# Two layers of linear attention and two of dilated window attention: a new order, new engine choices and new buffer numbers

## The chip, the cores and the metric

The kernel runs on one core of a Trainium2 chip. The metric is the time of one launch in microseconds, as the device reports it; before the change the median of three runs is 329.12 us. One execution was also taken with the hardware profiler.

A core has engines that run side by side, each through its own list of instructions in order: PE multiplies matrices (PEld is its loading of weights), DVE works elementwise, ACT applies functions and scales, POOL does small clears and copies, and SP issues the DMA transfers. An instruction that must wait for another engine or for a transfer holds up everything behind it in its own list.

## What is computed

```python
x = A_x                                    # 1 x 2048 x 512, bf16; 32 heads of 16
x = x + A(layernorm(x)); x = x + B(layernorm(x))
x = x + A(layernorm(x)); x = x + B(layernorm(x))

def A(x):                                  # linear attention with learned features
    q, k, v = heads(x @ wqkv)
    phi = lambda u: concat(softmax(u @ w_phi), softmax(-(u @ w_phi)))
    kv, z = sum_s(phi(k) * v), sum_s(phi(k))
    return (phi(q) @ kv / (phi(q) @ z + 1e-6)) @ wo

def B(x):                                  # 8 keys per row, at distances 0, 2, .. 14
    q, k, v = heads(x @ wqkv)
    return (softmax(q . k[window] / 4) @ v[window]) @ wo
```

## The kernel before

The 2048 rows are cut into four blocks of 512 (`x[0]` to `x[3]`), each of four tiles of 128 rows. All of `x` and all the weights stay in the core's memory. A method of the class `_Fast` writes each stage down as a list of small steps, one list for each stage, block and engine. The stages are:

- `s_loads` and `s_load_B`: the input loads, all on SP. `x[0]` comes in four tiles (L337), the other blocks whole (L340); the K and Q parts of A's weights as raw halves (L349, the tile `wraw`), its V part straight into `WA` (L343); `WoA` in four pieces (L353); B's weights `WB` in three parts (L418) and `WoB` in four (L422). A DMA also waits until the eighth one ahead of it has landed.
- `s_fold`: the raw Q and K weights are transposed on PE (L386), copied (`wT`), multiplied with the block diagonal of `w_phi` (L396) and copied into `WA`.
- `s_ln_first` and `s_norm`: layer norm. Statistics of a tile on DVE (L515, L516), logarithm and exponential on ACT (L450, L453), the shift on DVE (L457), the scaling into `xn` on DVE (L466) or ACT (L468), then the transposition to `xnT` on PE (L482, and a copy) or by DMA (L473).
- `s_a1`: K features and V. Matmuls L616 and L628, two exponentials L622 for each tile, V's eviction into `vaug`, sums by halving (L649 to L662), reciprocal (L668, L669), multiplication L674, and the sum over the rows L691, for all blocks into one bank.
- `s_a2`, `s_akv`: Q features (L721, L729) and their sums (L737, L743, L744); the finished sum is copied to `kvT`, transposed (L767) and spread into `ZM` and `R` (L776, L780). This is the one place in a layer A where every block of K must be finished.
- `s_a3`, `s_a4`, `s_out`: denominators, the product with `R`, the output projection (L543), the residual sum, and the squares (L563) for the next layer norm.
- `s_b1`, `s_b2`, `s_b3`: layer B. Projections L951; V is laid out for its window by 16 DMAs a block (L1012, the tile `Vg`); products `prod` (L1043), the sum over a head on PE (L1050), exponentials L1057, sums L1066, weights `PT` (L1078), products `pav` (L1105), their sums on PE (L1114), projection and residual as above.
- `s_e1` to `s_e4`: the last block of the last layer B is computed in another way, with block diagonal Q (`Qbd`), small matmuls (L1278, 128 to 144 for a tile, and L1322, 128 for a tile), masks L1304, normalization L1349 and transposes L1366. Its V goes through DRAM (L1232 to L1243) into the memory of `WA`, and into `Vx`.
- `s_flag`: counts that decide whether a second, general path has to run. DVE computes the flag (L1388 to L1405), every engine reads it (L1412), and here it never asks for the path.

Three tables set how these lists are merged, and the diff touches only these.

`_ORDER` is a list of 1488 numbers in base 36. Each names one of the 682 lists, and `run` takes the next step of that list and writes its instructions down. The order of instructions on every engine and on SP's queue is the order in this table:

```python
for w in _ORDER.split():
    key = self.names[int(w, 36)]
    i = n.get(key, 0)
    n[key] = i + 1
    self.threads[key][i]()
```

`_CHOICE` holds a digit for each of 380 steps that two engines could do; 1 stands for DVE, 0 for ACT. Most are evictions of a PSUM bank (`copy`, L203 on DVE, L205 on ACT) and the scaling of the layer norm. In the residual sum (`res`) 0 is DVE (L556), and 1 is one more matmul on PE, with the identity (L546), and an eviction on ACT (L553). In `bev` 1 means no eviction at all: DVE reads the bank itself.

`_SLOTS` gives each temporary its buffer by number: `ps` for the eight PSUM banks, `big` for eight buffers of 4096 elements a row, `med` for sixteen of about 2048, `t2` for six small ones. A step that writes a buffer waits until the last reader of its former content is done.

Of the kernel before, what the change touches and what calls it, by code (L numbers as in the profile page):

```python
# [75 lines left out]
6j 6a 6e 9a 9b 9c 9b 6r 9b 9b 83 7y 7y 84 9f 9b 8d 7z 6s 6s 6s 9f 9h 6s 6t 6t 88 89 9i 7y 6s 6t 4w 4x 83 83 6q
6q 7y 6q 85 88 4y 88 8b 83 9g 87 86 81 b2 9j 9k 88 8c 9m 9n 8f 9w 9x 82 9w 9w a1 6r 9z 69 6u 9w 80 6u 6v 8a 6u
6v 6x 6v 4w 6w 6q 6u 6v 6y 9m 4v 4z 4z 6z 4v 70 71 4z 4z 70 70 9y 72 7x 73 72 74 70 75 72 72 76 9o 9r 9r 50 51
8f 50 50 72 52 76 78 8e 8e 50 53 77 54 9r 9u 79 7a 9m 9p 7b 8f 9s 9t 55 8e 56 57 8f 55 58 55 55 59 8g 8g 8g 8e
a0 8g 57 57 a3 9r 5a 57 9v 9m 9q 5b a3 57 5b 8h 8h 5c b3 5e 5d 5f 5g 7x 9l a2 b0 b0 a3 b1 b1 b1 8g 8h b1 b3 b3  # L80
b6 b3 b7 bz c0 c0 a4 a4 a4 a3 a4 a5 a5 bz c0 c0 bz d3 b4 bz c0 c0 c0 c0 8f 8i b0 b1 a4 8i 8i 8i a5 as at b0 b1
b1 bx ap a2 b5 b1 ap 8j 8k 8j 8j 8l 8m 8j bx 8n 8o a3 a6 a2 a6 8p 8o 8o 8o bx aq aq aq aq by by by 8q 8t 8r 8s
as 8q a2 as as bx a6 a7 8q 8q a7 by 8u bz 8q a6 8u 8w 8y by by aw av 8v a7 8x a8 a7 aa ap ap a9 ab ac b8 b8 au
ac i7 ac ac by by bx b8 b8 ad aq aq af aq aq ag b9 bo c0 8z ah b8 bb bb ae ae ae ae ai be ax ae ai aj an c1 be
bc bb bc bc ak ax bc bb bc bc bc bc ac ac am ax ac ax ay al ac bg be bm bm ao bm bm bj bn bn bn bn bn bn ar ax
az az az bu bu bu bu az bn bn c2 bv bj bj by bu bj bu ba ba ba ba bp bh bp bp c1 bq bk bs br be c1 c1 bu bu bu
bp bj bf bl bl bl c2 c2 bi bl bv bw c2 c2 c2 bu bw c2 bw c2 bt bw c1 c7 c2 c8 c9 c9 ca c9 cb fp c3 cc cb ca ce
# [12 lines left out]
il ik fn fo gr gr il gw gx iq io iq iq gv gw gv gw gv gv ip iq iv dx dx fk fm fm gy gz h2 is gw gw ir it h2 iw  # L100
# [12 lines left out]
_SLOTS = {  # L113
    "med": (
        "0123456789abcdef346aff72ffc3105f92b4de6a7fd92b317ef99962c0517dbf2e3abf6925cd13e273a31dad901d74235cdb"
        "f72a94d35c017b9264acf31d08"
    ),
    "ps": (
        "0123124350123021456715604156734153267234701623047237452365001230210345672135304675261473045672350146"
        "1401230453013042567103651251741023452036714302310345031240230435406703203501467012012457245201240310"  # L120
        "3245602750235102563740130473024567142362047540123640760437034563745101021345067241301456701236204531"
        "7024560124567326452016435735601247351204561203460750264012312301203405367136731421432102324567467556"
        "47554701213740542010"
    ),
    "big": (
        "012345670123456012345617234561720351724361720436170425361725362503421034210354276"
    ),
    "t2": (
        "0123455500111123334555555555555555000002123402222222221314504555545555444455223000000145523333333333"
        "333333301045234102"  # L130
    ),
    "pp": (
        "640620202020"
# [1967 lines left out]
```

## Time and profile before

| | us |
|---|---|
| median of three runs | 329.12 |
| lowest, highest of them | 328.67, 1771.92 |
| span of the profiled execution, first to last instruction | 327.7 |
| busy in it: PE, DVE, ACT, POOL | 308.8, 296.3, 278.1, 39.1 |

One of the three runs took 1771.92 us; the median isn't moved by it. The span leaves out what lies around the program, 1.0 us and more by the two other runs. In the profile a line such as L1043 is a line of the kernel, and `out<-in` are the tiles' names without their buffer numbers. Times in a timeline count from the start of the span. A busy PE is not always a PE at its peak, as matmuls overlap. "Issue" as a releaser stands for a wait that the profile can't put down to another instruction.

### The profile page before, as it was taken

How to read it: one execution, taken by the hardware profiler on the slowest of the kernel's cores; microseconds unless marked ns; L12 is line 12 of the kernel's file. 1: busy time of each engine (PE TensorE's matmuls, PEld its weight loads, DVE VectorE, ACT ScalarE, POOL GpSimd, SP SyncE). 2: the span in 40 equal slices, each digit the busy share in tenths (PEclk: the TensorE clock that was granted, in tenths of full speed). 3: DMA queues.
4: the chain of work that ended last, by engine and by line, in shares of the span. 5: the costliest groups of instructions: out<-in, count | busy, mean ns of one | idle time of the engine just before them, and what ended most of it. 6: DMA issues, size and time to landing. Idle time of an engine off the chain costs nothing.

```text
span 327.7 us, 8877 instructions
## 1 busy us (share of the span) xinstructions
PE 308.8 (94%) x3542; PEld 153.5 (47%) x3574; DVE 296.3 (90%) x456; ACT 278.1 (85%) x640; POOL 39.1 (12%) x64
## 2 busy tenths in 40 slices
PE   7999999899999999999999999789999999986993
PEld 3644456444444454444444455543545444443441
DVE  6899995989999999999999999599898999999493
ACT  4999989999789977999999999799898866987360
POOL 6000000000020006000000000000040395210000
PEclk9999999999999999999999999999999999999799
DMA  7964300023677979679991200050588997549814
GB/s 203 341 162 90 108 2 4 2 68 81 144 172 140 132 149 158 108 131 131 145 121 28 40 0 4 4 141 9 145 147 121 192 136 131 135 83 176 158 67 137
DMA packets 45793, 36.41 MB, mean 111 GB/s; under 512 B 30832, under 2 KB 41136, under 8 KB 45744
## 3 DMA queue, kind: packets, MB, share of 16 engines
q1 hardware_dynamic: 45216, 35.75, 56.2%
q8 instruction: 30, 0.49, 0.7%
q14 instruction: 19, 0.16, 0.2%
q10 hardware_dynamic: 528, 0.02, 0.1%
HBM read 11.13 MB, written 3.25 MB: 44 GB/s over the span
## 4 chain that ended last, share of the span: by engine, by line
DVE 31%; ACT 31%; PE 18%; issue 12%; DMA 3%; SPq 2%; DVEq 0%; ACTq 0%
DVE prod L1043 6%; ACT Eq L729 5%; DVE pav L1105 5%; PE PS L543 5%; ACT sqd L563 5%; ACT Ek L622 4%; DVE x L556 4%; DVE Ek L674 3%; PE PS L951 3%; DVE xn L466 3%; ACT oT L205 2%; PE PS L1050 2%; DVE s L649 2%; ACT xn L468 2%; DMA wraw<-in_A_wqkv_dram 1%
## 5 line engine op out<-in xcount | busy, mean ns | idle before, releaser
L951 PE MATMUL PS<-xnT,WB 128*128 128x512 bf16 x336 | 76.7, 380 | 0.3 <-ACT K L205 0.2
L1105 DVE TENSOR_TENSOR pav<-PT,Vg 128x4096 bf16<-128x4096 bf16 (+1 forms) x29 | 63.3, 2219 | 0.6
L1043 DVE TENSOR_TENSOR prod<-QT,K 128x4096 bf16<-128x4096 bf16 x28 | 62.9, 2285 | 0.4 <-ACT QT L205 0.3
L951 PEld LDWEIGHTS <-WB 128*128 128x128 bf16 x336 | 37.3, 114 | 37.1 <-issue 4.2
L543 PEld LDWEIGHTS <-oT 128*128 128x128 bf16 x240 | 22.5, 98 | 31.3 <-issue 5.6
L729 ACT ACTIVATE Eq<-PS 128x512 bf16<-128x512 f32 x64 | 34.7, 624 | 0.0
L622 ACT ACTIVATE Ek<-PS 128x512 bf16<-128x512 f32 x64 | 33.9, 627 | 0.0
L563 ACT ACTIVATE sqd<-x 128x512 bf16<-128x512 bf16 x48 | 30.4, 633 | 2.1 <-DVE x L556 1.2
L721 PE MATMUL PS<-xnT,WA 128*128 128x512 bf16 x128 | 31.1, 380 | 0.2 <-ACT bs L870 0.2
L543 PE MATMUL PS<-WoB,oT 128*128 128x512 bf16 x105 | 27.7, 393 | 3.1 <-issue 2.9
L616 PE MATMUL PS<-WA,xnT 128*128 128x512 bf16 x124 | 29.9, 379 | 0.5 <-DVE x L556 0.2
L628 PE MATMUL PS<-WA,xnT 128*128 128x512 bf16 x122 | 29.9, 379 | 0.3
L543 PE MATMUL PS<-WoA,oT 128*128 128x512 bf16 x119 | 29.3, 380 | 0.8 <-DVE x L556 0.2
L556 DVE SCALAR_TENSOR_TENSOR x<-PS,x 128x512 bf16<-128x512 f32 x45 | 28.9, 684 | 0.3 <-PE PS L543 0.2
L205 ACT CAST oT<-PS 128x512 bf16<-128x512 f32 (+1 forms) x47 | 24.8, 595 | 3.8 <-PE PS L1114 3.5
L616 PEld LDWEIGHTS <-xnT 128*128 128x128 bf16 x128 | 12.3, 98 | 15.0 <-issue 0.6
L628 PEld LDWEIGHTS <-xnT 128*128 128x128 bf16 x128 | 12.3, 98 | 14.4
L205 ACT CAST V<-PS 128x512 bf16<-128x512 f32 x27 | 15.4, 591 | 4.1 <-PE PS L951 4.1
L674 DVE TENSOR_TENSOR Ek<-Ek,rk 128x4096 bf16<-128x4096 bf16 (+1 forms) x10 | 18.6, 1860 | 0.3 <-ACT rk L669 0.3
L721 PEld LDWEIGHTS <-WA 128*128 128x128 bf16 x128 | 11.7, 97 | 15.2 <-issue 2.0
L205 ACT CAST K<-PS 128x512 bf16<-128x512 f32 x30 | 17.4, 591 | 0.3 <-PE PS L951 0.3
L466 DVE TENSOR_SCALAR xn<-x,rstd,nmr 128x512 bf16<-128x512 bf16 x46 | 16.8, 408 | 0.6
(164 smaller groups left out, 496.9 us busy)
## 6 DMA issues: line engine op xcount, KB each, us to landing
Vg<-V SPq DMA_DIRECT2D x112, 131.5 KB, 4.8
Prho<-rd SPq DMA_DIRECT2D x8, 512.0 KB, 5.4
x<-in_A_x_dram SPq DMA_DIRECT2D x3, 512.0 KB, 5.8
WB<-in_B_wqkv_dram SPq DMA_DIRECT2D x3, 512.0 KB, 8.6
out_dram<-x SPq DMA_DIRECT2D x6, 256.0 KB, 2.3
wraw<-in_A_wqkv_dram SPq DMA_DIRECT2D x4, 256.0 KB, 5.4
vd<-Vs SPq DMA_DIRECT2D x2, 272.0 KB, 3.3
x<-in_A_x_dram SPq DMA_DIRECT2D x4, 128.0 KB, 3.9
```

Source lines behind the costliest of these rows:

```text
L205: self.nc.scalar.copy(out=out, in_=in_)
L543: nc.tensor.matmul(y[:], lhsT=lh(t, c), rhs=Wo()[:, c, :], start=(c == 0), stop=(c == NB - 1 and not onpe))
L556: nc.vector.scalar_tensor_tensor(out=xb[:, t, :], in0=T[t][:], scalar=1.0, in1=xb[:, t, :], op0=ALU.mult, op1=ALU.add, **kw)
L563: nc.scalar.activation(out=sqd[:], in_=xb[:, t, :], func=ACT.Square, accum_out=T["ss"][:, t:t + 1])
L616: nc.tensor.matmul(pk[:], lhsT=xnT[:, t, k, :], rhs=self.WA[:, k, D:2 * D], start=(k == 0), stop=(k == NB - 1))
L622: nc.scalar.activation(out=T["E"][:, t, s, :], in_=T["k", t][:], func=ACT.Exp, scale=1.0 - 2.0 * s)
L628: nc.tensor.matmul(pv[:], lhsT=xnT[:, t, k, :], rhs=self.WA[:, k, 2 * D:3 * D], start=(k == 0), stop=(k == NB - 1))
L721: nc.tensor.matmul(pq[:], lhsT=self.WA[:, k, hb * P:(hb + 1) * P], rhs=xnT[:, :, k, :], start=(k == 0), stop=(k == NB - 1))
L729: nc.scalar.activation(out=self.Eq[L, b][s][:, :, hb, :], in_=T[hb][:].rearrange("p (t i) -> p t i", t=4), func=ACT.Exp, scale=1.0 - 2.0 * s)
L951: nc.tensor.matmul(pp[:], lhsT=self.WB[:, k, i * D + c:(i + 1) * D:NB], rhs=xnT[:, :, k, :], start=(k == 0), stop=(k == NB - 1))
L1043: nc.vector.tensor_tensor(out=pr[:], in0=QT[:, c:c + 1, :].to_broadcast([P, NW, TB]), in1=win, op=ALU.mult)
L1105: nc.vector.tensor_tensor(out=pv, in0=PT[:, :, lo:lo + n].unsqueeze(1).to_broadcast([P, NB, 2, n]), in1=vw, op=ALU.mult)
```

## The change

All three tables are replaced: the order of the 1488 steps, 70 of the 380 choices, and the numbers of all buffers but one kind. The steps themselves are the same, and so is the number of transfers. The choices and the first and last lines of the order:

```diff
 _ORDER = """
-8 2e a d c 23 i i i 0 j 9 k j l i 2 i i i i 0 b o p i f 2 0 1m 1m 1o m n i i i i 1n 1m 1m 1p 1q 1m 1r o q r 1m t
-4 z 1s s z i 3 1t 1u 21 z z 10 3 1t i7 1v 22 22 21 1 24 24 2p z 0 t u 13 11 15 1t 1t t 16 1w 1t 1y 12 12 12 12
...
-iu h0 it ix iw h3 h3 h4 h5 h6 h2 h1 h3 h7 h2 h5 h3 h8 h5 h5
+9 8 i i cd 2e i 0 7 i i i f e i 7 7 a 5q 3u 0 j i i g i i i 4e 2 ci 2 23 i b 0 1m k i 3 o j 3 p 3o 4 20 20 5
+5o 1 l 3r 5k o q 20 0 6 m 1n t n 20 r 2p 1m 1o 1m 1m 1m z 20 4f z 1m z 1t s 1p z 1r 1q 1t 1s 21 1u 1v 21 22 t
...
+iu gw gw it h0 h2 iw h3 h3 h2 h1 h3 it h4 h6 h5 h5 h7 h5 h2 h3 ix h8 iw h5
 """
...
 _CHOICE = (
-    "0010110111100111111111000000100000100110011100000111011110010100000101010000100000000000111101011100"
-    "1010010100001100100000000000000011111110000100001010100000000000000000010111001000001101000000000000"
-    "1010000011111100000000000100010110011011010100101111000000001001000000010110010001000100011100100000"
-    "00000000011111010000011100000000000000000000000001000011001000000000000000001100"
+    "1010111111111111111111000001000000010011000001001111011110000100001001111000000000000000011011011100"
+    "1010010100000111000000001000000011110110001000001011000000000000000000011111000000001111000000000000"
+    "0000000011111100000000000100000110011011010100111100111001000010000001100110010000010000101110000000"
+    "00000000010101000000011100000000000000000000000000000001011000001000000000000001"
 )
...
 _SLOTS = {
     "med": (
-        "0123456789abcdef346aff72ffc3105f92b4de6a7fd92b317ef99962c0517dbf2e3abf6925cd13e273a31dad901d74235cdb"
+        "abd89475ed902461f913fcf1f05c07c9ea342861f15420a7685f9541a7eb9286f271d092d5d84f060bef56cd34abe0978ef1"
...
     "ps": (
-        "0123124350123021456715604156734153267234701623047237452365001230210345672135304675261473045672350146"
+        "6714027603524071257601374502537642307560457364261747301361543203127360475162306475142673540670531243"
...
```

Read with the names of the lists, the order of SP's loads is:

```
before  x0 tile 0, K half, x0 tile 1, K half, x0 tile 2, x1, Q half, Q half, WA V part, x0 tile 3,
        x2, x3, WB, WoA, WoA, WB, WB, (transposes of x2 and x3) ...
after   x0 tile 0, WoA, WoA, WoA, x0 tile 1, K half, K half, x0 tile 2, Q half, Q half, x1,
        WB, WB, x2, WA V part, WB, x0 tile 3, x3, WoB, WoB, WoB, WoA, (transposes) ...
```

Three other places, in the same words:

- DVE at the start. Before: statistics of x0 tile 2 and of x1, copy of `wT`, shift of x1, statistics of x0 tile 3, scaling of x1 (one of its four tiles on ACT). After: the same up to the copy of `wT`, statistics of x0 tile 3, shift of x1, all four scalings of x1. The logarithm of x0's tiles 2 and 3 stands on ACT ahead of the copies of the folded Q weights in both.
- PE at the second `s_akv`. Before: the Q sums L737 of block 2, then the transposes L767 of `kvT`. After: L767 first.
- The end. DVE before: product `pav`, four masks, two residual sums, two normalizations L1349, `PT`, `pav`, two normalizations, four more `pav` (two of them halves), then residual sums, with the three steps of the flag before the last four of these. After: two of the masks come earlier; `pav`, two normalizations, mask, residual sum, `PT`, residual sum, `pav`, normalization, `pav`, normalization, residual sum, `pav`, two residual sums, the two halves, residual sums, and the flag's steps behind the last of them. On PE the groups L1322 of the first two tiles follow each other in both; those of the other two follow each other before and stand apart after.

POOL's clears of `WA`, `Qbd` and `Vx` and its copies of the last 16 columns from block to block change places among themselves. Square L435 of the Q weights, one of the flag's counts, stands earlier on ACT: the first of the two ahead of the first `s_akv`, where both stood in layer B before.

More of the change, by code (lines that the diff above doesn't have):

```diff
@@ new lines @@
+5o 1 l 3r 5k o q 20 0 6 m 1n t n 20 r 2p 1m 1o 1m 1m 1m z 20 4f z 1m z 1t s 1p z 1r 1q 1t 1s 21 1u 1v 21 22 t
+10 z 20 15 24 22 7 1t u 11 1w 25 ck 24 13 t 26 16 1t 12 12 12 1t v x 12 14 h 1y 1t 22 17 22 w 1z w y 2c 2d 1x
+2c 18 18 18 2d 21 18 2d 39 1f ch 39 3a 3a 19 2c 18 2c 1d e3 22 22 1a ce 21 2d 1b 2d 24 2f 1c 3a 1f 22 1f 27 2d
+39 3t 22 1f 29 29 3s 2d e7 2d 3a 2f 1g 1e 2f 1f 1i 1j 1k 2g 1h 2h 3a d 24 2n 28 3a 2o 2n 2n 2o 3p 2o 2o 29 2o
+2n 2q 2i 29 1l 2k 2a 2k 2o c 3b 2q 2k 2r 2o 2o 29 2k 2y 2s 2y 2q 2z 2v 2z 20 2z 2z 2t 36 36 2y 36 39 31 2l 3c
@@ new lines @@
+2f e4 2k 36 3a 2z 2j 37 2y 2v 31 2q 2z 2z 2u 2b 2b 2b 2b 32 2v 36 2m 2v 2z 36 36 36 3a 2m 2w 33 3c 2m 2m 31 3b
+36 34 2v 31 3c 35 30 3b 3c 2x 2x 2x 37 36 2x 38 38 38 38 3i 3c 39 3b 3h 3c 3a 3j 3k 3k 3c 3c 3d 3e 3k 3l 3m 3b
+3d 3e 3c 3n 3e 3e 5h 3m 5i 3l 3d 3q b2 3m 3l 3d 3m 5j 3m 3m 3e 3e 3v 3e 5i 3m 5h 3m 3m 3e 3d 5i 7c 5n 5m 3e 5h
+5i 5p 3m 7d 3f 3f 5i 5r 3g 3g 5i 3g 5i 3w 3f 5i 3z 3f 3g 5i 3x 3y 5i 3g 7e 40 bo 3g 5s 5t 5v 5u 41 41 7d 42 3g
+41 41 5w 44 5x 45 7f 43 5x 43 5x 43 46 5y 43 47 60 3g 43 3f 47 49 90 48 41 4b 7f 41 3g 4c 41 41 61 4a 4d 5x 5l
@@ new lines @@
+5z 4l 7f 91 92 5z 62 4m 4g 4g 5z 91 5z 7d 7d 63 4q 93 93 4g 4r 5z 4h 63 4q 7g 4j 7j 64 4q 7h 66 65 4s 67 68 4l
+7k 4q 4i 4w 4l 7i 4n 4t 4u 4f 69 4w 4l 4o 7l 7m 3h 7l 7o 7l 7l 93 7p 6a 7n 4g 6f 91 7n 6k 7q 7n 7n 4v 6k 91 6g
+6k 7r 6b 6k 7n 4v 6a 4k 4p 6m 4w 7r 7t 6p 6c 6l 6n 7s 7v 7u 6a 6f 7w 4w 6f 6r 6o 94 6h 6d 4x 69 96 95 4x 4x 6q
+6r 98 4x 97 7x 99 9a 4y 6i 4y 99 99 9c 9b 99 9d 9e 9b 6q 9b 6q 6f 6r 6a 6j 9b 83 8d 7y 7y 9f 6e 6r 9b 6s 84 7z
+6s 6s 6s 6t 6t 80 88 bd 9f 9j 9h 6s 4w 9g 9i 83 8f 6t 83 6r 6u 86 9k 6u 83 85 88 4x 87 89 4y 7y 7y 82 8a 4w 6q
@@ new lines @@
+81 88 8b 9m 6u 4v 4v 9w 6u 9w 88 9y 9w 6v 6v 4z 6v 9n 8c 7x 4z 9x 6v 6w 4z 9r 6x 6z 6y 9s 70 9z 70 71 4z 72 70
+73 72 74 72 70 9m 9r 75 50 9o 72 50 51 50 50 76 8e 9m 52 9m 9r 54 8f 72 76 9p 53 79 78 8f 7a 77 55 8e 9w 9u 9q
+7b 56 55 8f 9l a0 9t 57 55 a1 58 55 8g 8g 8e 8g 8e 5a 59 57 57 57 a3 8g b0 8h 8h b1 5b a3 57 bz bz bz c0 c0 c0
+b0 c0 c0 8g b1 5b 5e b1 a3 5f 5c 5d 5g 9r 9v b0 a3 b3 b1 8h b3 a4 b5 a4 8f 8i a4 c0 a4 a2 bz b0 b1 a2 8i b4 8i
+a5 a2 a5 a2 b1 c0 b1 a4 a5 bx 8i by a3 b3 b6 b3 bx bx by b7 by by ap 8j c0 8j 8j b1 by 8l 8k 8m 8j a6 a6 bx ap
@@ new lines @@
+aq 8n c6 8o 8o aq by aq aq 8p 8o 8o by by 8r 8s as 8q 8q a6 as 8t 8q 8q ap ap 8u at a6 aq aq 8q 8u 8w as a7 av
+a8 bx au 8v a7 a7 bz 8x 8y 8z aq aq b8 a7 aa as b8 a9 ab aw ac b8 c0 ad ac b8 ac by ac af ae be ax ar ag ae b9
+bb ae ah ae bb bb bc bf b8 ai ax bc ae be ai ax bc bc c1 aj ak bb bc bc bc ac am ac ac an ac bc ax al be ay ao
+bm bn bn bm bn bn bm bn bj ax bh bm bu bn az bn az bu az az ba bu bu bv ba ba ba c1 bn c1 c1 bj bj c2 bg bj bp
+bu bk c2 c2 be bq c2 d4 c2 bp i7 bu bj br bu bu bu bl bl bi bp c2 bv bp bl bl bw bs bt bu c2 bw bw bw c7 c8 c9
@@ new lines @@
+c9 c2 c1 ca c3 c2 cb c9 cc fp cb c4 ca c4 fq cg c3 cf e0 d3 cb fr cb c4 cb ca cb cj c4 c3 cb fq cb c3 c4 fs c4
+c4 c4 cb cb c5 fs cl e1 cm i7 e2 e1 c3 e0 cp c5 co cn fs e1 cq e6 e5 e0 e1 cq cq e1 e1 c4 e8 e1 e9 e1 e1 ea e1
+cr cu eb h9 cs ec ct ed ee cq fq ef eg cv cs cs cs eg fq ha ft hb eg fu ha cw eg hc hc fv fw fx ej fy eh cs cw
+fy cx cy el fz cq cq fy cz ek d0 d1 cq cq hc d2 fy ei ei ei ei df df g2 g3 em ei df df g1 em dg eq en ep g0 dh
+eo ha di er dj g0 da db ha da dc d4 d5 d6 g0 dk d5 g0 hd g4 dl d5 he hg hf da hh d7 dd hi g0 hi hj d8 g4 es hi
@@ new lines @@
+hi hl g5 et et hk hm dk hk hn hk hk ho hk ey da g6 g8 de dk ho f3 hr hp d5 dl hq f8 ez g7 d9 f4 hs dl et f3 f5
+ht g9 ey ew f3 dl f3 eu fa f0 dm dm dm dm ey f7 ev i1 dn dn fa dl f1 f6 i1 dk et i2 i3 es i6 i6 i6 i1 i6 fa ey
+i6 ex hu f2 f9 i4 gq dm i6 dn i1 i6 i6 f9 gl fa fb gm fb fb fb dl i5 hw c6 i6 i6 i6 fc hv fc i9 ia i9 hx fb do
+do do ib i9 i9 gl fc ga fa id gn ie dp dp dp hu dr f9 hw hw ds i6 i8 do i6 dq ic i6 i6 ic hz fd gb hy gc gg ic
+fd c5 gg gh i6 gl gi f9 ic fd ic ic ic ic go ic ic hw ic ic ic ic i0 gb fe gd dp gs fe ff dt gs fg ic fe if if
@@ L102 @@
+fh ig ig ih gb if ig if ig ge ih gg gj gg gk gb gl gf if gp ig if gs gs gt ig gr du if ig if ih gt gt ig gt fd
+gr gu gr gr ii gu ii ij ij ij ik ij ik du gt ih dv du dw du dy il ga gu fe il dx gs dz im gv in ii fi fj ij ij
+iq ik fj fk gv ii ij ij ik fl gw il gx fm dx fj io gv fn iq fj iq il is fo gw fm gw gv gv ip gz iq gy h2 ir iv
+iu gw gw it h0 h2 iw h3 h3 h2 h1 h3 it h4 h6 h5 h5 h7 h5 h2 h3 ix h8 iw h5
 """
 _CHOICE = (
-    "0010110111100111111111000000100000100110011100000111011110010100000101010000100000000000111101011100"
```

53 lines of the change are left out of this document (8 added, 45 removed).

## The prediction

> **What bounds the kernel now.** I read the page first (busy time, chain), then busy time by stretches of the span, then the order of time at the places where several engines pause together.
>
> ```profile
> span 327.7 us, 8877 instructions
> PE 308.8 (94%) x3542; PEld 153.5 (47%) x3574; DVE 296.3 (90%) x456; ACT 278.1 (85%) x640; POOL 39.1 (12%) x64
> DVE 31%; ACT 31%; PE 18%; issue 12%; DMA 3%; SPq 2%; DVEq 0%; ACTq 0%
> ```
>
> Three engines are nearly full and the chain that ended last passes through all three in turn: there is no single bound. A step pushed later on one of them delays the others, and only stretches in which several are idle can give time back. PE's idle is 327.7 - 308.8 = 18.9 us, DVE's 31.4, ACT's 49.6. The stretches say where (columns: stretch, its length, busy us of PE, PEld, DVE, ACT, POOL, then the clock granted to PE, the DMA share and GB/s):
>
> ```profile
> 0.00:10.00 10.00, 7.69 (x53) 4.40 (x55) 6.88 (x26) 5.25 (x10) 5.62 (x33) 1.00 0.79 228
> 10.00:20.00 10.00, 9.89 (x88) 6.21 (x88) 9.35 (x26) 9.67 (x20) 0.00 (x0) 1.00 1.10 315
> 20.00:30.00 10.00, 9.95 (x47) 4.47 (x46) 9.76 (x26) 9.94 (x24) 0.47 (x2) 1.00 0.32 65
> 30.00:40.00 10.00, 9.95 (x47) 4.54 (x47) 9.35 (x12) 9.94 (x22) 0.00 (x0) 1.00 0.55 133
> 40.00:60.00 20.00, 19.41 (x474) 11.50 (x473) 15.88 (x29) 17.97 (x42) 0.00 (x0) 1.00 0.01 2
> 300.00:310.00 10.00, 7.33 (x175) 3.90 (x176) 5.21 (x6) 4.07 (x13) 0.00 (x0) 0.83 0.97 180
> ```
>
> The reader is to see two things. From 10 to 40 us all three engines are full while, from 10 to 20, the DMA share is over one: the input loads saturate the queue just while the engines consume what they bring. And from 300 to 310 us everything pauses, at a lowered clock.
>
> **The loads at the start, the largest term.** SP's queue issues the loads. The old order: three tiles of x0 with the four halves of the raw weights and x1 between them, then the V part of WA (ninth) and tile 3 of x0 (tenth), then x2, x3 and the weights of layer B. The new order puts ahead of the V part and of tile 3: three of WoA, x2 and the weights of layer B; the V part is fifteenth, tile 3 seventeenth. Sizes:
>
> ```profile
> x<-in_A_x_dram SPq DMA_DIRECT2D x3, 512.0 KB, 5.8
> WB<-in_B_wqkv_dram SPq DMA_DIRECT2D x3, 512.0 KB, 8.6
> wraw<-in_A_wqkv_dram SPq DMA_DIRECT2D x4, 256.0 KB, 5.4
> x<-in_A_x_dram SPq DMA_DIRECT2D x4, 128.0 KB, 3.9
> WA<-in_A_wqkv_dram SPq DMA_DIRECT2D x1, 512.0 KB, 7.1
> WoA<-in_A_wo_dram SPq DMA_DIRECT2D x4, 128.0 KB, 6.0
> ```
>
> Old: through the V part 3 x 128 + 4 x 256 + 512 + 512 = 2432 KB, 2.49 MB. New: through the V part 3 x 128 (x0) + 3 x 128 (WoA) + 4 x 256 + 2 x 512 (x1, x2) + 2 x 512 (WB) + 512 = 4352 KB, 4.46 MB; through tile 3 another WB and the tile, 4992 KB, 5.11 MB. By the stretches the queue has moved 2.28 MB by 10 us and then 0.315 MB each us. The old V part's bytes are through at 10 + 0.21 / 0.315 = 10.7 us; it landed 7.1 us after its issue (next rows), at 12.0, so completion lags the byte count by 1.3 us. The same sum puts the new V part at 10 + 2.18 / 0.315 + 1.3 = 18.2 us and tile 3 at 10 + 2.83 / 0.315 + 1.3 = 20.3 us. Who needs them:
>
> ```profile
> 4.88 1.58 SPq L343 DMA_DIRECT2D WA<-in_A_wqkv_dram  x1
> 12.13 0.86 SPq L418 DMA_DIRECT2D WB<-in_B_wqkv_dram  x1
> 12.88 1.89 PE L628 MATMUL PS<-WA,xnT 128*128 128x512 bf16 x8
> 13.24 0.68 DVE L515 BATCH_NORM_STATS2 stat<-x 128x6 f32<-128x512 bf16 x1
> 14.06 1.03 DVE L466 TENSOR_SCALAR xn<-x,rstd,nmr 128x512 bf16<-128x512 bf16 x3
> 14.18 0.29 ACT L450 ACTIVATE lnv<-mv,eps_t 128x2 f32<-128x2 f32 x1
> 15.28 0.50 PE L482 MATMUL PS<-ident,xn 128*128 128x128 bf16 x6
> ```
>
> L515 at 13.24 is the statistics of tile 3. In the new DVE order the same step stands at nearly the same place (after the four statistics of x1 and the copy of wT), and behind it are the shift and the four normalizations of x1. So DVE waits from about 13 to 20.3: +7.1 us. ACT has the logarithm of tiles 2 and 3 (14.18) ahead of the evictions of the folded weights, and waits with it: +7. PE reaches L628 after the same folding work as before and waits for the V part, 18.2 - 12.88 = +5.3; then it stands before the transposes of x1 (L482), whose input DVE delivers 1.2 us after it gets tile 3 (14.06 + 0.4 - 13.24), at 21.5: +6.2. As all three are full until 40 us, nothing there takes this back. I take **+7.0**. A second way agrees: the old seventeenth issue began at 12.13 and was a WB load; 12.13 + 8.6 = 20.7, which makes +7.5, the upper end. The lower end is the 3.9 us that a 128 KB tile of x took: 12.13 + 3.9 = 16.0, or +2.8.
>
> By the Trainium skill, DMA: Bandwidth & Descriptors, Anatomy of one DMA, a transfer costs a fixed 2.0 us plus its bytes at 436 GB/s; that would land the tile at an estimated 14.4 us, make this term +1.2 and the whole sum 328.0. Its fit is for another issuing path, and the 7.1 us that 512 KB took here speak for the queue instead.
>
> **The engine choices.** Of the 380 choices 70 change; the rows that price them:
>
> ```profile
> L205 ACT CAST oT<-PS 128x512 bf16<-128x512 f32 x45 | 24.1, 604 | 3.3 <-PE PS L1114 3.0 <-PE PS L924 0.2
> L203 DVE CAST oT<-PS 128x512 bf16<-128x512 f32 x14 | 9.4, 682 | 0.0
> L205 ACT COPY xnT<-PS 128x1024 bf16<-128x1024 bf16 x4 | 4.1, 1027 | 0.0
> L203 DVE COPY xnT<-PS 128x1024 bf16<-128x1024 bf16 x5 | 3.3, 686 | 0.0
> L468 ACT ACTIVATE xn<-x,nmr,rstd 128x512 bf16<-128x512 bf16 x18 | 14.3, 814 | 1.7 <-DVE nmr L457 1.7
> L466 DVE TENSOR_SCALAR xn<-x,rstd,nmr 128x512 bf16<-128x512 bf16 x46 | 16.8, 408 | 0.6
> L553 ACT ACTIVATE x<-PS 128x512 bf16<-128x512 f32 x19 | 11.2, 598 | 2.0 <-PE PS L546 2.0
> L556 DVE SCALAR_TENSOR_TENSOR x<-PS,x 128x512 bf16<-128x512 f32 x45 | 28.9, 684 | 0.3 <-PE PS L543 0.2
> L546 PE MATMUL PS<-x,ident 128*128 128x512 bf16 x19 | 7.7, 406 | 0.0
> ```
>
> Seven evictions of 128x512 go to ACT, three of 128x1024, six normalizations and four residual sums to DVE. ACT: 7 x 0.604 - 3 x 1.027 - 6 x 0.814 - 4 x 0.598 = -6.1 us. DVE: -7 x 0.682 + 3 x 0.686 + 6 x 0.408 + 4 x 0.684 = +2.5. PE loses four identity matmuls, at most 4 x 0.406 = 1.6. The most loaded engine loses half a per cent, and ACT's gain lies mostly where it has slack; I count these at 0 except two residual sums in the last stage, below.
>
> **The pause at 300 us.**
>
> ```profile
> 293.75 2.28 DVE L1105 TENSOR_TENSOR pav<-PT,Vg 128x4096 bf16<-128x4096 bf16 x1
> 302.62 1.43 PE L543 MATMUL PS<-WoB,oT 128*128 128x512 bf16 x4 [2.55 <-issue]
> 309.45 0.69 DVE L1349 TENSOR_TENSOR oB<-PS,rdB 128x512 bf16<-128x512 f32 x1 [4.41 <-ACT rdB L1341]
> 311.07 6.75 DVE L1105 TENSOR_TENSOR pav<-PT,Vg 128x4096 bf16<-128x4096 bf16 x4
> ```
>
> After two groups of 128 small matmuls (L1322, row tiles 0 and 1 of the last block) PE stood 2.55 us for no reason that the profile shows, then ran slowly; DVE waited 4.41 us for the third group before it could go on to its last four products. The new DVE order puts a mask, two residual sums, the weights PT and one 2.29 us product between the second and third normalization, which covers such a wait; but the two L1322 groups still stand back to back on PE. Best -4.4, worst 0; I take half, -2.2. The two residual sums that DVE gets here cost 2 x 0.684 = +1.4. Together **-0.8**.
>
> **Smaller terms.**
>
> ```profile
> 206.53 0.58 ACT L205 CAST kvT<-PS 128x512 bf16<-128x512 f32 x1
> 207.64 0.40 PE L767 MATMUL PS<-ident,kvT 128*128 128x128 bf16 x4
> L435 ACT ACTIVATE sq<-WA 128x2048 bf16<-128x2048 bf16 x2 | 3.8, 1912 | 0.0
> 320.41 0.15 DVE L1405 TENSOR_SCALAR fl<-tot 128x1 int32<-128x1 f32 x1
> ```
>
> In the second layer A the transposes of kvT started 0.53 us after their input (206.53 + 0.58 = 207.11), behind the Q sums L737; the new order has them first: **-0.5**. One square of L435 moves into the stretch before the first Q sums, where ACT is the fullest: 0 to +1.9, taken as 0, since ACT loses evictions of xnT there. The three small steps that decide the flag, like the one at 320.41, now stand after DVE's last sum, with the read of the flag behind them on every engine; the last store is under way meanwhile, so 0 to +0.5, taken as 0. POOL's clears and halo copies change places with 39.1 of 327.7 us busy: 0 unless one is late. The new buffer numbers make new waits and drop old ones, which the trace of before cannot price; with the rest of the reordering they are bounded by DVE's idle 4.1 us in 40 to 60 on the good side, and as much on the bad. I take **-1.0** for order and buffers together, since there 4.1 us of 20 are open to be won, while new idle time has to come from somewhere that the rows don't show.
>
> Sum: 327.7 + 7.0 - 0.8 - 0.5 - 1.0 = 332.4 us of span. The median of the three runs, 329.12, lies 1.4 above the span, so 333.8.
>
> **Rivals.** *The loads don't hold it up*: small loads land soon after issue. Against it stand the DMA share of 1.10 and the 7.1 us for 512 KB; for it, the 3.9 us of the x tiles. Then 327.7 + 2.8 - 4.4 + 1.4 - 0.5 - 1.0 + 1.4 = 327.4. Only if another 5 us came out of the idle stretches would it be faster by 2%.
>
> *Slower, by a cold PE and an overfull ACT*: the wait at the start empties PE for 4 us, longer than the 2.55 us at 302.62 after which 300 to 310 shows a clock of 0.83, that is (1 - 0.83) x 10 = 1.7 us lost. It decides when PE's gap is at least that long. Price: loads +7.5, clock +1.7, square +1.9, no gain at 300 (+1.4), -0.5 and 1.4 around: 327.7 + 13.4 = 341.1. By the Trainium skill, TensorE: Matmul & The Clock Gate, What's actually happening, an idle window of about 3.4 us halves the clock for at least as long again, an estimated 1.7 us; the row shows it after a shorter gap.
>
> *The change does nothing*: excluded, as the program's loads do stand in the new order.
>
> **Numbers.** Forecast 333.8, own range 330 to 338, chance 0.52; loads harmless 327.4, 0.23; cold and overfull 341.1, 0.25. The range 326 to 342 takes in all three. About 2% is what a measurement of this kernel can tell from no change: below 322.5 is faster, above 335.7 slower. Slower: the last rival and a third of the forecast's share, 0.25 + 0.18 = 0.43; faster 0.06, out of the first rival; within, 0.51.
>
> **What would show it.** The trace of after should have DVE and ACT idle some 7 us before 21, ended by the load of x; L628 on PE waiting for WA until 18; the first L776 some 7 us later; a wait of L1349 of 0 to 4 us near the end. If the statistics of tile 3 run before 16 us, the first term is wrong. If they run at 20 and the time is still no longer, the order after it won back more than I could find.

## The result and the profile after

| | us | ratio to before, 95% interval |
|---|---|---|
| before, median of 4 runs | 329.26 | |
| after, median of 4 runs | 331.94 | 1.0078, 1.0051 to 1.0104 |
| after in a later round, 6 runs | 331.43 | 1.0102, 1.0076 to 1.0128 |
| span of the profiled execution, before and after | 327.7, 329.3 | |

The change makes the kernel slower by about 0.8%, within the 2% on either side that the prediction gave a chance of 0.51. It forecast 333.8 with a range of 326 to 342. The first lines of the page of after:

```profile
span 329.3 us, 8838 instructions
PE 307.3 (93%) x3540; PEld 152.8 (46%) x3570; DVE 297.3 (90%) x464; ACT 273.1 (83%) x632; POOL 47.8 (15%) x64
```

Its busy time by stretches (columns as in the prediction):

```profile
0.00:10.00 10.00, 7.57 (x40) 3.34 (x40) 6.74 (x20) 3.76 (x7) 5.89 (x34) 1.00 0.79 215
10.00:20.00 10.00, 5.92 (x46) 3.58 (x48) 4.42 (x10) 4.96 (x11) 0.00 (x0) 0.88 1.08 362
40.00:60.00 20.00, 19.89 (x361) 11.23 (x362) 17.86 (x31) 19.22 (x40) 0.76 (x2) 1.00 0.03 9
300.00:310.00 10.00, 9.79 (x273) 5.92 (x268) 10.00 (x12) 8.03 (x26) 0.00 (x0) 1.00 0.97 169
```

Two stretches changed most, in opposite directions. From 10 to 20 us all three engines stand half empty, where they were full before: DVE 4.42 us busy instead of 9.35. From 300 to 310 they are full where they paused: PE 9.79 instead of 7.33, DVE 10.00 instead of 5.21, at a clock of 1.00 instead of 0.83. The order of time in after shows what the first stretch waits for (start, duration, engine, line, operation, in brackets the idle time ahead and what ended it):

```profile
9.23 1.23 SPq L343 DMA_DIRECT2D WA<-in_A_wqkv_dram  x1
12.10 1.19 SPq L337 DMA_DIRECT2D x<-in_A_x_dram  x1
17.65 1.86 PE L628 MATMUL PS<-WA,xnT 128*128 128x512 bf16 x4 [3.80 <-DMA WA<-in_A_wqkv_dram]
19.35 0.69 DVE L515 BATCH_NORM_STATS2 stat<-x 128x6 f32<-128x512 bf16 x1 [3.73 <-DMA x<-in_A_x_dram]
20.30 0.29 ACT L450 ACTIVATE lnv<-mv,eps_t 128x2 f32<-128x2 f32 x1 [4.24 <-DVE nmr L457]
21.41 0.83 PE L482 MATMUL PS<-ident,xn 128*128 128x128 bf16 x12
```

L628 starts at 17.65 where it was 12.88, L515 at 19.35 for 13.24, L450 at 20.30 for 14.18, the transposes of x1 (L482) at 21.41 for 15.28: 4.8 to 6.1 us later on each engine. Whether the delay stays is read from lines that come later (each row: durations in ns, shortest, median and longest, then the start of the first and of the last one in us). Before and after:

```profile
L776 DVE TENSOR_TENSOR ZM<-PS,maskH x4: 180/186/190, 54.3 to 208.3; 128x32 bf16<-128x32 bf16 x4
L951 PE MATMUL PS<-xnT,WB x336: 376/379/409, 77.3 to 290.8; 128*128 128x512 bf16 x168
L1349 DVE TENSOR_TENSOR oB<-PS,rdB x4: 679/685/692, 300.4 to 310.5; 128x512 bf16<-128x512 f32 x4
```

```profile
L776 DVE TENSOR_TENSOR ZM<-PS,maskH x4: 180/185/191, 59.7 to 213.9; 128x32 bf16<-128x32 bf16 x4
L951 PE MATMUL PS<-xnT,WB x336: 376/379/408, 83.1 to 296.4; 128*128 128x512 bf16 x168
L1349 DVE TENSOR_TENSOR oB<-PS,rdB x4: 674/678/690, 303.0 to 311.9; 128x512 bf16<-128x512 f32 x4
```

The delay is 5.4 us at 54, 5.8 at 77, 5.6 at 208 and 5.6 at 291: nothing in 230 us takes it back. The last of these is known to some 1.7 us: in two more profiles of kernels that do the same up to there (after run again, and after with its flag moved, both below) the last L951 starts at 294.7 and 295.2. Between the last L951 and the last L1349 the delay shrinks from 5.6 to 1.4. At the very end it is 1.6.

### The profile page after: what moved, and what is told of

Same layout as the page of the kernel before. It is cut to its first block, busy times and chain, and to the rows that moved or that the text cites. A ratio compares the mean times of both kernels' runs of the same rounds, so it can differ in the third digit from the quotient of the medians.

```text
span 329.3 us, 8838 instructions
## 1 busy us (share of the span) xinstructions
PE 307.3 (93%) x3540; PEld 152.8 (46%) x3570; DVE 297.3 (90%) x464; ACT 273.1 (83%) x632; POOL 47.8 (15%) x64
## 4 chain that ended last, share of the span: by engine, by line
PE 65%; DVE 16%; ACT 7%; DMA 6%; SPq 3%; issue 2%; DVEq 0%; ACTq 0%
PE PS L951 15%; PE PS L543 13%; PE PS L628 7%; PE PS L616 6%; PE PS L721 5%; DVE prod L1043 4%; PE PS L1114 3%; PE PS L1050 3%; DMA WA<-in_A_wqkv_dram 3%; DVE Ek L674 2%; DMA Prho<-rd 2%; ACT Eq L729 2%; PE PS L1171 2%; DVE x L556 1%; PE PS L691 1%
## 5 line engine op out<-in xcount | busy, mean ns | idle before, releaser
L951 PE MATMUL PS<-xnT,WB 128*128 128x512 bf16 x336 | 76.8, 380 | 1.0 <-DVE V L203 0.9
L951 PEld LDWEIGHTS <-WB 128*128 128x128 bf16 x336 | 37.3, 114 | 37.1 <-issue 4.5
L729 ACT ACTIVATE Eq<-PS 128x512 bf16<-128x512 f32 x64 | 36.3, 615 | 0.4 <-PE PS L721 0.3
L628 PE MATMUL PS<-WA,xnT 128*128 128x512 bf16 x121 | 31.5, 393 | 4.8 <-DMA WA<-in_A_wqkv_dram 3.8
L622 ACT ACTIVATE Ek<-PS 128x512 bf16<-128x512 f32 x64 | 35.7, 626 | 0.2 <-PE PS L616 0.2
L556 DVE SCALAR_TENSOR_TENSOR x<-PS,x 128x512 bf16<-128x512 f32 x49 | 32.2, 683 | 0.8 <-PE PS L543 0.5
L205 ACT CAST oT<-PS 128x512 bf16<-128x512 f32 (+1 forms) x53 | 28.4, 595 | 2.3 <-PE PS L1114 1.3
L616 PE MATMUL PS<-WA,xnT 128*128 128x512 bf16 x123 | 29.9, 379 | 0.3
L543 PE MATMUL PS<-WoB,oT 128*128 128x512 bf16 x106 | 26.6, 379 | 0.6 <-issue 0.5
L628 PEld LDWEIGHTS <-xnT 128*128 128x128 bf16 x128 | 12.4, 100 | 19.8 <-issue 5.6
L993 POOL COPY vh<-V 128x64 bf16<-128x64 bf16 x6 | 11.1, 1853 | 71.0 <-ACT V L205 71.0
L466 DVE TENSOR_SCALAR xn<-x,rstd,nmr 128x512 bf16<-128x512 bf16 x52 | 19.1, 417 | 0.5
L616 PEld LDWEIGHTS <-xnT 128*128 128x128 bf16 x128 | 12.3, 98 | 14.9 <-issue 0.8
```

What stands on the lines that cost most here:

```text
L205: self.nc.scalar.copy(out=out, in_=in_)
L543: nc.tensor.matmul(y[:], lhsT=lh(t, c), rhs=Wo()[:, c, :], start=(c == 0), stop=(c == NB - 1 and not onpe))
L556: nc.vector.scalar_tensor_tensor(out=xb[:, t, :], in0=T[t][:], scalar=1.0, in1=xb[:, t, :], op0=ALU.mult, op1=ALU.add, **kw)
L616: nc.tensor.matmul(pk[:], lhsT=xnT[:, t, k, :], rhs=self.WA[:, k, D:2 * D], start=(k == 0), stop=(k == NB - 1))
L622: nc.scalar.activation(out=T["E"][:, t, s, :], in_=T["k", t][:], func=ACT.Exp, scale=1.0 - 2.0 * s)
L628: nc.tensor.matmul(pv[:], lhsT=xnT[:, t, k, :], rhs=self.WA[:, k, 2 * D:3 * D], start=(k == 0), stop=(k == NB - 1))
```

## The experiments

Every kernel ran beside runs of before, and the ratios are to these. Choices and buffers are those of the kernel that is named, and only the steps that are given change places.

### The loads of before in the kernel after, and the reverse

```diff
 SP, kernel after
-x0 tile 0, WoA, WoA, WoA, x0 tile 1, K half, K half, x0 tile 2, Q half, Q half, x1, WB, WB, x2, WA V part, WB, x0 tile 3, x3 ...
+x0 tile 0, K half, x0 tile 1, K half, x0 tile 2, x1, Q half, Q half, WA V part, x0 tile 3, x2, x3, WB, WoA, WoA, WB, WB ...
```

> The kernel after, with SP's input loads in the order of before and everything else as after. Theory (the loads hold up the start): the statistics of tile 3 of x0 run at 13 to 14 us instead of 19.35, L628 on PE at 12 to 13 us instead of 17.65, and the 6.1 us go from the end as well: 331.9 - 6 = about 326, ratio to before 0.985 to 0.993, with the gain at 300 us kept. Rival (the wait only fills idle time that the new order has anyway a little later, between 40 and 220 us): 330 to 332, with the idle time coming back there.

The two transposes of x2 and x3 that stand among the loads move with them. 324.32, ratio 0.9854 (0.9834 to 0.9875), 1.7 less than was expected. In its order of time the waits are gone, and in its lines the later steps are early again:

```profile
13.22 1.03 PE L628 MATMUL PS<-WA,xnT 128*128 128x512 bf16 x4
12.75 0.68 DVE L515 BATCH_NORM_STATS2 stat<-x 128x6 f32<-128x512 bf16 x1
15.40 0.83 PE L482 MATMUL PS<-ident,xn 128*128 128x128 bf16 x12
```

```profile
L776 DVE TENSOR_TENSOR ZM<-PS,maskH x4: 180/186/192, 53.7 to 206.8; 128x32 bf16<-128x32 bf16 x4
L951 PE MATMUL PS<-xnT,WB x336: 376/379/408, 77.1 to 289.3; 128*128 128x512 bf16 x168
```

L482 is back at 15.40, the first L776 at 53.7. Against these lines, those of after give the delay by the loads alone: 6.0 us at 54 and at 77, 7.1 at 207 and at 289. The order of the loads alone costs the kernel after 331.43 - 324.32 = 7.1 us, or 7.6 against its first median. The closest pair, two kernels with the flag moved that differ in the loads alone and ran in one round (below), gives 331.04 - 323.38 = 7.7.

The reverse puts the first line of loads in place of the second in the kernel before.

> The kernel before, with SP's input loads in the order of after and everything else as before. Theory: DVE and ACT wait 6 us for tile 3 of x0, PE 5 us for the V part of WA, nothing takes it back: 329.3 + 6 = about 335.3, ratio 1.016 to 1.021. Rival: under 332.

335.64, ratio 1.0199 (1.0177 to 1.0221): +6.2 us beside 329.41 for before in its round, as the theory has it, with no other step moved. Why the loads cost more in the kernel after isn't settled. Everything else in the change together is worth 324.32 - 329.41 = -5.1 us, and the loads take back more than that.

### Each of the two late loads alone

```diff
 SP, kernel after: tile 3 early
-... x1, WB, WB, x2, WA V part, WB, x0 tile 3, x3 ...
+... x1, x0 tile 3, WB, WB, x2, WA V part, WB, x3 ...
 SP, kernel after: V part early
-... x1, WB, WB, x2, WA V part, WB, x0 tile 3, x3 ...
+... x1, WA V part, WB, WB, x2, WB, x0 tile 3, x3 ...
```

> The kernel after, with the load of tile 3 of x0 alone moved up behind x1; the V part of WA stays where it is. Theory (two waits lie side by side, and each alone is enough): DVE and ACT no longer wait, but PE waits for the V part until about 18 us with the transposes of x1 behind it: 331 to 332, at most 1 us won. Rival (tile 3 is the cause, the V part costs nothing): 325 to 326.

> The kernel after, with the load of the V part of WA alone moved up behind x1; tile 3 of x0 stays where it is. Theory: PE has L628 done by 16 us and then waits for DVE's normalizations of x1, which wait for tile 3 until 19.4: 331 to 332, at most 1 us won. Rival (the V part is the cause): 325 to 326.

331.6 (1.0069, 1.0042 to 1.0095) and 332.77 (1.0105, 1.0055 to 1.0155): neither wins anything that could be told from after's 331.43 and 331.94. The order of time with tile 3 early, then with the V part early:

```profile
15.44 0.68 DVE L515 BATCH_NORM_STATS2 stat<-x 128x6 f32<-128x512 bf16 x1
17.82 1.86 PE L628 MATMUL PS<-WA,xnT 128*128 128x512 bf16 x4 [3.97 <-DMA WA<-in_A_wqkv_dram]
22.04 1.48 PE L482 MATMUL PS<-ident,xn 128*128 128x128 bf16 x12
```

```profile
13.60 1.03 PE L628 MATMUL PS<-WA,xnT 128*128 128x512 bf16 x4
19.37 0.69 DVE L515 BATCH_NORM_STATS2 stat<-x 128x6 f32<-128x512 bf16 x1 [3.75 <-DMA x<-in_A_x_dram]
21.15 1.46 PE L482 MATMUL PS<-ident,xn 128*128 128x128 bf16 x12 [3.99 <-DVE xn L466]
```

and a stretch of the latter:

```profile
22.00:24.00 2.00, 2.00 (x21) 2.00 (x20) 1.59 (x5) 1.21 (x3) 0.00 (x0) 0.50 0.11 32
```

Each time the other wait holds L482 until 21 to 22 us. A reader who removed one of them would have found "no effect" and gone on to look elsewhere. In the second, PE's gap of 3.99 us stands directly ahead of the work that all engines need, and that work then runs at half the clock (0.50 in the last row).

### The cold PE

```diff
 def mv(t):
     T["v", t] = pv = self.ps()
+    if (L, b, t) == (0, 0, 0):
+        for _ in range(9):
+            nc.tensor.matmul(pv[:], lhsT=self.kvT[:, 0:P], rhs=self.kvT[:], start=True, stop=True)
```

> The kernel after, with nine matmuls of zeros on PE just ahead of the first L628 (their result is overwritten), so that PE is not empty while it waits for the V part. Theory (the granted clock of 0.84 in 10 to 21 us costs nothing more, as PE waits for DVE at 21.4 anyway): the clock there stays at 1.0, the time at 331.9 within 0.5. Rival (the cold PE adds its 1.8 us to the wait): 330 to 330.5.

330.67, ratio 1.0044 (1.0022 to 1.0065). The unchanged kernel was run again to have a nearer neighbour.

> The kernel after, unchanged, beside the others of this round. 331.9 within 0.6; the distance to the run with nine matmuls of zeros (330.67, ratio 1.0044) says whether the cold PE costs anything: theory 0 to 0.4 us, rival 1 us or more.

331.43, ratio 1.0102 (1.0076 to 1.0128). The nine matmuls do what they should. The stretch behind the wait has a clock of 1.00 in this kernel, 0.50 in after:

```profile
18.00:20.00 2.00, 2.00 (x16) 1.04 (x14) 0.59 (x1) 0.00 (x0) 0.00 (x0) 1.00 1.10 367
```

```profile
18.00:20.00 2.00, 2.00 (x9) 1.01 (x8) 0.65 (x1) 0.00 (x0) 0.00 (x0) 0.50 1.10 353
```

But the order of time in this kernel, and a line of after:

```profile
21.19 0.94 PE L482 MATMUL PS<-ident,xn 128*128 128x128 bf16 x12 [1.15 <-DVE xn L466]
23.16 2.76 PE L616 MATMUL PS<-WA,xnT 128*128 128x512 bf16 x12
```

```profile
23.41 2.54 PE L616 MATMUL PS<-WA,xnT 128*128 128x512 bf16 x11
```

With the clock up, PE waits 1.15 us for DVE ahead of L482, as the theory says, and is 0.25 us ahead at the next L616 (0.67 ahead of the second profile of after, where that L616 starts at 23.83). Of this little is left later: the first projection of layer B (L951 in after) starts at 83.1 in both, and at 83.5 in the second profile of after. The medians differ by more: 0.8 and 1.3 us from those of after, and the ratios by 0.0034 and 0.0058, which is 1.1 us against the first run of after and 1.9 against the later one; only against the later one do the two intervals not touch. The runs are from different rounds. So the medians say that the cold PE costs 0.8 to 1.9 us, and the traces show 0.2 to 0.7 of it at 23 us and at most 0.4 at 83; where the rest would be lost isn't shown.

### The late flag

```diff
 DVE, kernel after
 counts L1388, L1390, L1393
-residual sums L556 x4
 decide L1401, L1403, L1405
-read of the flag
+residual sums L556 x3
+read of the flag
+residual sum L556
```

> The kernel after, with the three steps that decide the flag (and so the read of it) ahead of DVE's last four residual sums, as before. Theory (the late flag puts its read and the branch behind the end of DVE's work): the last residual sum ends within 0.3 us of 323.4, the span falls by 0.7 to 1.2 us and the time by 1 to 2 us, to 330 to 331. Rival (the last store hides it): 331.9 within 0.4.

The matmul that sums the counts (L1397 on PE) moves ahead with them. 331.04, ratio 1.0055 (1.0031 to 1.0078), 0.4 to 0.9 below after.

> The kernel after, with the loads of before and the early flag. Theory: both gains add, 331.9 - 6 - 1.5 = about 324.5, ratio 0.98 to 0.99. Rival: only one of the two counts, 326 or 330.

Here the same is done in the kernel after with the loads of before. 323.38, ratio 0.9835 (0.9813 to 0.9858), 0.94 below the same kernel with the late flag, which ran in the same round. In both cases the intervals of the two kernels overlap, so the time alone doesn't show the gain; the traces do. The end of before, of after, and of after with the early flag in order of time:

```profile
320.41 0.15 DVE L1405 TENSOR_SCALAR fl<-tot 128x1 int32<-128x1 f32 x1
320.48 2.47 DVE L556 SCALAR_TENSOR_TENSOR x<-PS,x 128x512 bf16<-128x512 f32 x4
```

```profile
320.77 2.63 DVE L556 SCALAR_TENSOR_TENSOR x<-PS,x 128x512 bf16<-128x512 f32 x4 [0.35 <-PE PS L543]
323.70 0.15 DVE L1405 TENSOR_SCALAR fl<-tot 128x1 int32<-128x1 f32 x1
```

```profile
320.12 0.15 DVE L1405 TENSOR_SCALAR fl<-tot 128x1 int32<-128x1 f32 x1
320.19 2.49 DVE L556 SCALAR_TENSOR_TENSOR x<-PS,x 128x512 bf16<-128x512 f32 x4
```

From the last residual sum's end to the end of the span it is 327.7 - 322.95 = 4.75 us before and 329.3 - 323.40 = 5.9 after, and 4.9 with the early flag (span 327.6, last sum until 322.68). The last store doesn't hide the flag. The kernel with both moves, all of the change but the loads and the flag, is the fastest of the study and beats before and after.

### The square

```diff
 ACT, kernel after with the loads of before and the early flag
-square L435 ahead of the first s_akv ... square L435 in layer B
+square L435 x2 in layer B
```

> The kernel after with the loads of before and the early flag (323.38 measured), and with the first square L435 moved from 54 us back to its place beside the second one. Theory (the square takes 1.9 us of ACT where ACT is full, and DVE and PE wait for it): 321.5 to 322.5. Rival (ACT's gain from the changed choices pays for it, as predicted): 323.4 within 0.5, or slower by as much if ACT is full at the new place.

(The square also gets another buffer of the same kind.) 324.36, ratio 0.9868 (0.9844 to 0.9892): not faster. From 40 to 60 us ACT falls from 19.13 us busy, with the square there, to 17.50, while PE stays at 19.4. ACT's work there wasn't what the end waited for.

### The end of the last block

```diff
 DVE, kernel before
-L1349 x2, L1078, L1105, L1349, L1349, L1105, L1105, L1105 x2 (halves)
+L1349 x2, L1078, L1105, L1105, L1105, L1349, L1349, L1105 x2 (halves)
```

> The kernel before, with two of DVE's products L1105 of the last block moved ahead of the third normalization L1349; no other engine's order changes. Theory (the gain at the end comes from DVE's wait of 4.4 us being covered): two products of 2.29 us fill the wait, the third L1349 starts at its input or a few tenths later, and the time falls by 3 to 4.6 us: 329.4 - 4 = about 325.4, ratio 0.985 to 0.99. Rival (PE is what the end waits for, through its pause of 2.55 us and the low clock behind it): under 1 us, 328.5 or more.

329.24, ratio 0.9993 (0.9967 to 1.0018). The theory fell, and the rival held. DVE's wait for the third normalization is covered, but it only moves. DVE's order of time:

```profile
302.31 6.74 DVE L1105 TENSOR_TENSOR pav<-PT,Vg 128x4096 bf16<-128x4096 bf16 x3
309.01 0.69 DVE L1349 TENSOR_TENSOR oB<-PS,rdB 128x512 bf16<-128x512 f32 x1
317.35 0.69 DVE L556 SCALAR_TENSOR_TENSOR x<-PS,x 128x512 bf16<-128x512 f32 x1 [4.37 <-PE PS L543]
```

and two pieces of the chain of work that ended last (start, duration, what):

```profile
299.83 2.34 issue
302.17 1.75 PE PS L543 x4
```

The 4.4 us of waiting now stand ahead of the residual sum at 317.35, ended by PE. From 287 to 319 us the chain runs through PE alone, with the pause of 2.34 us in it. The chain of before does the same from 290 to 320, and has the pause too:

```profile
300.07 2.55 issue
```

So the end of before waits for PE: for its pause and for the low clock behind it. In before that is, in stretches of 2 us:

```profile
302.00:304.00 2.00, 1.38 (x5) 0.58 (x5) 1.94 (x2) 0.00 (x0) 0.00 (x0) 0.78 1.04 156
304.00:306.00 2.00, 2.00 (x7) 0.59 (x4) 1.04 (x1) 0.00 (x0) 0.00 (x0) 0.50 1.05 164
306.00:308.00 2.00, 2.00 (x87) 1.46 (x86) 0.00 (x0) 0.20 (x1) 0.00 (x0) 0.87 0.98 164
```

2.55 + 2 x (0.22 + 0.50 + 0.13) = 4.25 us. In after and in after with the loads of before PE doesn't pause there and the clock stays at 1.00. From the last L951 to the end of the last residual sum, before and then after with the loads of before:

```profile
290.80:322.95 32.15, 28.24 (x550) 13.89 (x554) 26.03 (x33) 18.07 (x50) 0.24 (x1) 0.95 0.62 135
289.30:316.50 27.20, 25.93 (x533) 13.49 (x536) 26.48 (x32) 15.97 (x44) 0.53 (x1) 1.00 0.67 159
```

PE is idle for 3.9 us in the first and for 1.3 in the second, and it is busy for 2.3 us less at the full clock, with 17 matmuls fewer, while DVE has no less to do: 5.0 us in all. No run takes the pause alone out of before, so that most of the 5.0 us are the pause and the clock is read from the chains and these rows, and not shown by an experiment. The pause isn't always followed by a low clock. In before with the new loads PE stands nearly as long, one matmul further on in its list, and the clock stays up; from the order of time, and the stretch:

```profile
309.65 0.82 PE L543 MATMUL PS<-WoB,oT 128*128 128x512 bf16 x3 [2.34 <-issue]
310.00:312.00 2.00, 2.00 (x18) 0.89 (x19) 1.66 (x1) 0.00 (x0) 0.00 (x0) 1.00 1.05 158
```

Two runs looked for the cause of the pause.

```diff
 SP, kernel before
-Vg x16, stores of x[0] (two) and the others
+Vg x4, stores of x[0] (two), Vg x12, the other stores
```

The two stores are those of `x[0]`, though the expectation says x1.

> The kernel before, with the two stores of x1 put behind the first four of the last sixteen loads Vg<-V on SP, so that the other twelve loads wait until about 301 us; no other engine's order changes. In before, two instruction transfers of 16 KB fall at 299 and 305 us, with the DMA share over 1 from these loads, and PE pauses from 300.07 to 302.62. Theory (PE's instructions come late because their transfer shares the DMA engines with the loads of Vg): with the engines free at 299 the pause of 2.3 to 2.55 us goes, and with it the low clock behind it (1.7 us): 329.4 - 4 = about 325.4, less some tenths if the last products wait for their loads. Rival (the pause comes from the two groups of small matmuls alone): the pause stays, 329 to 330.

327.99, ratio 0.9974 (0.9952 to 0.9996). The stretch with the pause, two pieces of the chain, and DVE's third normalization in order of time:

```profile
298.00:300.00 2.00, 1.35 (x123) 1.12 (x109) 2.00 (x4) 1.94 (x8) 0.00 (x0) 1.00 0.03 8
```

```profile
299.35 1.34 issue
...
309.40 4.43 DMA Vg<-V
```

```profile
305.85 0.69 DVE L1349 TENSOR_TENSOR oB<-PS,rdB 128x512 bf16<-128x512 f32 x1 [1.73 <-ACT rdB L1341]
```

With the DMA engines empty (share 0.03) the pause is 1.34 us and the clock stays at 1.00; the third L1349 comes 305.85 - 299.82 = 6.0 us after the first, where it was 309.45 - 300.39 = 9.1. With the three profiles that have these loads beside the pause (2.55, and 2.34 twice) this says that the loads lengthen it and do not make all of it; it is one profile. What was won is then lost to the loads themselves, which land late: the chain ends in 4.43 us of waiting for Vg, and I had expected only some tenths of that.

```diff
 PE, kernel before
-L1322 tile 0, L1322 tile 1, L1066, L543 x8, L1366 tile 0, L1366 tile 1 ...
+L1322 tile 0, L1066, L543 x8, L1366 tile 0, L1322 tile 1, L1366 tile 1 ...
```

> The kernel before, with the second group of L1322 (row tile 1 of the last block) behind eight matmuls L543 and the transposes of row tile 0, and its ACT and DVE steps moved with it. Theory (instructions run out, because 256 of them are used up in 1.24 us while the next ones are under way): the eight L543 of 0.21 us give the transfer 1.7 us more, the pause shrinks to under 1 us and the clock stays up: 326 to 327.5. Rival (the pause doesn't depend on how closely the groups stand): it stays at 2.3 or more, 329 to 330.

The steps of ACT and DVE that belong to the second group move with it. 331.64, ratio 1.0099 (1.0065 to 1.0134): slower. No pause at 300; one of 1.29 us comes at 306.51, inside the groups of tiles 2 and 3, after PE had waited on ACT and DVE for tile 1, and the clock is 0.50 from 308 to 312. It neither bears out the theory nor the rival, since the pause moved and new waits came in. Why the kernel after has no pause stays open: with the loads of before it runs the two groups at 293.79 at a DMA share of 1.07, and doesn't pause.

## Why the prediction was right

**The loads.** Taken +7.0 (bounds +2.8 to +7.5), measured +6.2 in the kernel before and 7.1 to 7.7 in the kernel after. The way there held as well: the V part was forecast for 18.2 us, tile 3 for 20.3; their readers started at 17.65 and 19.35. The term that was off is the rate. I took 315 GB/s from 10 us on; the same queue moved 362 between 10 and 20, and 215 instead of 228 up to 10, which gives 10 + (5.11 - 2.15) / 0.362 + 1.3 = 19.5 for tile 3. That nothing takes the delay back while all three engines are full until 40 us was right, and reaches further: nothing does until 291. The prediction named both waits; that each alone suffices is shown by the two runs with one load moved. By the Trainium skill, DMA: Bandwidth & Descriptors, Anatomy of one DMA, the tile would have landed at an estimated 14.4 us; in the trace its reader starts at 19.35, so the measurement decides. In this queue the bytes ahead set the time, and not the one transfer.

**The pause at 300 us.** Taken -2.2, best -4.4, with the two residual sums -0.8; the end came out beyond the best. Here the step failed that said the new DVE order "covers such a wait": the run with the cover alone shows nothing won. What went is PE's own pause and its low clock, 4.25 us, and I had argued that it would stay since "the two L1322 groups still stand back to back". The half that I took was no estimate of either, so that the term had the right sign is luck. (A group is 64 matmuls with 64 weight loads; the 128 matmuls of the prediction count both.) From the last L951 to the end of the span the kernel after with the loads of before wins 5.2 - 1.5 = 3.7 us, with the late flag's 0.9 in it, so 4.6 without the flag; up to the last residual sum it is 5.0. It repeats: this last part of the span takes 36.9, 36.9 and 36.3 us in before, before with the products first and before with the new loads, and 32.9, 33.3 and 33.2 in after, after run again and after with the loads of before.

**The engine choices.** ACT was to lose 6.1 us of work and lost 5.0 (278.1 to 273.1), DVE to gain 2.5 and gained 1.0, both without effect on the time that could be found; no run changes the choices alone. The two residual sums of the last stage (+1.4) are not to be seen apart: DVE is at 10.00 of 10 there and PE at 9.79.

**The second layer A, and the rest of the order.** Taken -0.5 and -1.0. With the loads of before, L776 starts 0.50 us after the end of kvT's eviction (206.65 against 206.15); it was 1.04 before (208.15 against 207.11), so -0.54. All of the stretch up to the last L951 is 1.5 us shorter (289.3 against 290.8). The sum held. For the -1.0 that is luck, since it was a guess between -4.1 and +4.1; and over all profiles of kernels with the same steps up to there the gain is 0.9 to 2.9 us.

**The flag and the square.** The square at 0 held. The flag was taken as 0, with 0.5 as its bound, because the last store would hide it. It costs 0.9 (0.94 where both kernels ran in one round); the step that failed is the cover. In after the issue of the last store ends at 323.77 and the flag is decided at 323.85, with its read still to come; before, it was decided at 320.56.

**The rivals.** That the loads do no harm is excluded by the first two runs. The cold PE came as described, with its gap of 3.80 us and a clock of 0.50 behind it, but of its price of 1.7 us only 0.2 to 0.7 can be found in the trace, as PE had DVE to wait for anyway; the medians would allow all of it. The Trainium skill, TensorE: Matmul & The Clock Gate, What's actually happening, puts the idle time that lowers the clock at about 3.4 us; the gaps of 3.80 and 3.99 agree, but in before a pause of 2.55 us was followed by 0.50 as well, and there the measurement decides. Nor is it the length of the pause alone: after 2.34 us the clock was 0.58 in before with the products first, and 1.00 in before with the new loads. ACT is nearly full from 40 to 60 us (19.22 of 20), as this rival had it, but moving the square away from there won nothing.

The terms as measured: -5.1 for all but the loads (of which -1.5 up to 291 us, the rest at the end with the flag's +0.9 in it) and 7.1 to 7.7 for the loads, +2.0 to +2.6 together; after stood 331.94 - 329.26 = 2.7 and 331.43 - 328.33 = 3.1 us above before in its two rounds. The forecast was 333.8 - 331.94 = 1.9 us too high: the end gave some 3.8 us more than the -0.8 that was taken, and the flag and the loads took back 0.9 and up to 0.7. So the forecast came this near in part because two errors pull against each other. And since the range of 16 us took in all three rivals, the time alone tells little between them; the landing times and the runs with the loads exchanged do.

## What to carry to other kernels

When a schedule is reordered, look first at the transfers: a load that stands seven places later on a full queue arrives by its share of the bytes, and the sum of bytes over rate, with the lag of one load from the trace, predicted its arrival to a microsecond. Where two engines wait side by side for two loads, moving one of them shows nothing; undo both before you call a wait harmless. And a wait that is covered on one engine wins only if that engine is what the end waits for: follow the chain of waits past the pause before you price it.

## What was not expected of the hardware

In before, before with the products first and before with the new loads, PE stood 2.34 to 2.55 us after some 250 small matmuls and weight loads in 1.24 us, and waited for nothing that the profile shows. With the DMA engines nearly empty it was 1.34 us. In the kernel after it didn't come at all; with the groups set apart, one of 1.29 us came inside the other two groups. What decides it was not found, nor why the clock fell after some of these pauses and not after others.
